# One-hot rows of a route ahead of its products, paired transposes for the logits, and other precedences in a planned kernel

## The chip, the core and the metric

The kernel runs on one core of a Trainium2 chip. The metric is the device time of one execution in microseconds (us). The engines of the core are TensorE (PE, matmuls), VectorE (DVE), ScalarE (ACT), GpSimd (POOL, which here gathers and scatters rows by index) and SyncE (SP, which here issues plain DMAs and DMA transposes). Each engine takes its own list of instructions strictly as the program puts it down, and waits on semaphores for the others.

## The reference, cut to what is computed

A convolution with softmax weights over 7 positions, then a mixture of 8 experts with the two best of each token, then a mixture with the best one. There are 2 x 3584 = 7168 tokens of width 192, and 1024 hidden columns.

```python
def _attn_ref(x, weight_gen):                     # x (2, 3584, 192), weight_gen (2, 3584, 8, 7)
    w = np.exp(weight_gen - np.max(weight_gen, axis=-1, keepdims=True))
    w = w / (np.sum(w, axis=-1, keepdims=True) + 1e-09)
    ...
    return np.einsum('bshk,bskhg->bshg', w, x_unf).reshape(B, S, D)

def _moe_ref(x, w_gate, w_noise, noise, w1, w2):
    noisy_logits = x @ w_gate + np.log1p(np.exp(x @ w_noise)) * noise
    top2 = np.argpartition(-noisy_logits, 2, axis=1)[:, :2]
    ...
            h = np.maximum(x[mask] @ w1[e], 0.0)
            out[mask] += top2_w[mask, k, None] * (h @ w2[e])

def _moe2_ref(x, w_gate, w1, w2):
    expert_idx = np.argmax(x @ w_gate, axis=1)
    ...
        out[mask] = gate_w[mask, None] * (np.maximum(x[mask] @ w1[e], 0.0) @ w2[e])
```

## The kernel before

**Phases and blocks.** Tokens are held in tiles of 128 rows. The expert work is split into five phases: phases 0 to 2 are the first mixture (the tokens in three parts), phases 3 and 4 the second (two parts). Within a phase the tokens of an expert are packed into blocks of 128 rows, and one or two blocks make a unit. A unit is a gather on POOL (`gt<-rows,src`: rows by index into SBUF), a DMA transpose on SP (`xt<-gt`), and then on PE, for each block, the first layer (`ph`, 40 matmuls of 128 columns, or 40 of 256 for two blocks) and the second (`py`, 24 matmuls of 192 columns). Between them ACT makes `hh` and DVE makes `hl` (high and low part of the hidden values, one `hl` for each 512 values of `ph`). The result `yo` is scattered by POOL, to `ybuf` in the first mixture and to `out_dram` in the second. `w` holds weights that are copied in for blocks whose expert is known only at run time, `wres` the resident ones.

**The route.** Before a phase can start, its route has to know where each token goes: `msk` (one-hots of the chosen expert), two products and two scans over it, a block and a place for each token, and then the inversion, token numbers by place. The inversion is a sum of one-hot products: for groups of 8 columns (`OG` = 8) DVE makes `pex` (the place as a one-hot row) and `bex` (the block as one, times a code; two instructions), and PE multiplies them into `pr`. From `pr`, after a product with `lost`, come `src` (the row numbers for POOL's gathers), then `ge` and the block's experts. `pex` and `bex` have two buffers each (`EB` = 2). The function is `route_`, the loop is that over `groups`.

**Logits.** Before a route come the logits of its tokens. A sub is up to four tiles of 128 rows. When its rows are final (`finish` for the convolution, `settle` after the first mixture), they are stored to memory and queued. `turn_thread` has SP transpose the rows two tiles at a time (`TPN` = 2) into `xtg`, of which there are three (`XR` = 3), and `logit_thread` multiplies them by the gate's weights on PE (`pm`). The function of a sub's convolution is `conv_lane`, which ends in `finish`.

**The order.** All this is written as generators ("threads") under one planner, `Feed`. After each step of PE's main loop it asks each thread when its next step could start by a model of the engines' clocks, adds a number of the thread's own ("late", negative for precedence), and takes the smallest. A thread tells what its step needs with `yield engine, tiles`: the step then counts as ready when the engine is free and the tiles are. The planner runs when the program is built. What it decides is the fixed order of every engine's list. `started` is filled when the first phase begins its expert work; all that is ahead of it is called the start here.

## Time and profile before

| | |
|---|---|
| median of 3 executions | 1036.34 us |
| lowest, highest | 1026.44, 1036.35 us |
| the profiled execution | 1031.08 us |
| its span | 1029.3 us |
| mean granted TensorE clock | 0.936 of full speed |

The span is the profiled stretch of one execution; some 1.8 us of the execution lie around it. All rows below come from that one execution, which is 5.3 us quicker than the median of the three and 4.6 us slower than the lowest. A row names a line, an engine, an operation, and out<-in by the program's names; L189 is a helper that records every instruction, so that nearly all have its line and the names tell them apart. In the timeline the brackets at the end of a row hold the engine's idle time ahead of it and what ended that.

### The profile page before, as it was taken

The page shows a single profiled execution, that of the slowest core. Times are in us where ns is not written, and L with a number is a line of the kernel's source. Part 1 is how long each engine was busy: PE and PEld are TensorE (multiplying, and loading weights), DVE is VectorE, ACT ScalarE, POOL GpSimd, SP SyncE. Part 2 cuts the span into 40 slices and gives each one's busy share as a digit, 9 for nine tenths or more (in the row PEclk, how much of TensorE's full clock was granted, in tenths as well). Part 3 has the DMA queues.
Part 4 walks back from the last instruction along what each step waited for, and adds up shares of the span by engine and source line. Part 5 has one row for each costly group of instructions (what it writes and reads, how often), then busy time and mean ns, then how long its engine had stood idle before and what let it go on. Part 6 is the DMA issues. An engine that isn't in the chain of part 4 may idle for free. (4 is left out here: it accounts for less than half of the span.)

```text
span 1029.3 us, 26213 instructions
## 1 busy us (share of the span) xinstructions
PE 885.5 (86%) x10130; PEld 816.2 (79%) x10130; DVE 741.6 (72%) x1818; ACT 500.9 (49%) x1003; POOL 424.5 (41%) x575
## 2 busy tenths in 40 slices
PE   1995369999995999999679999998399999999985
PEld 0553259989995899999579988998298998999985
DVE  7686859899985998958565767758686879355442
ACT  1343049674441544556255876865084733344332
POOL 3020044555525455533343444443145544465542
PEclk8897579999997999999889999999599999999998
DMA  9256089979843877644499999995289876563592
GB/s 286 54 137 150 0 164 261 220 191 177 188 87 77 155 146 168 172 103 134 118 159 254 261 232 236 245 254 98 59 183 198 194 149 200 112 121 87 176 255 82
DMA packets 246369, 168.30 MB, mean 164 GB/s; under 512 B 177564, under 2 KB 228079, under 8 KB 246236
## 3 DMA queue, kind: packets, MB, share of 16 engines
q1 hardware_dynamic: 227500, 121.68, 53.3%
q0 software_dynamic: 18736, 44.85, 18.0%
q8 instruction: 83, 1.36, 0.6%
q14 instruction: 50, 0.41, 0.2%
HBM read 74.46 MB, written 32.59 MB: 104 GB/s over the span
## 5 line engine op out<-in xcount | busy, mean ns | idle before, releaser
L189 ACT ACTIVATE hh<-ph 128x512 f16<-128x512 f32 x362 | 214.3, 594 | 344.6 <-PE ph L189 303.1
L189 PE MATMUL ph<-xt,wres 128*128 128x256 f16 (+1 forms) x3200 | 327.1, 255 | 31.1 <-DMA xt<-gt 19.6
L189 DVE SCALAR_TENSOR_TENSOR hl<-ph,hh 128x512 f16<-128x512 f32 x362 | 245.3, 685 | 136.7 <-ACT hh L189 132.2
L189 PEld LDWEIGHTS <-wres 128*128 128x128 f16 x3200 | 266.2, 100 | 53.1 <-issue 29.7
L189 PE MATMUL py<-wres,hh 128*128 128x192 f16 x2048 | 271.9, 246 | 4.7 <-ACT yo L189 4.6
L189 PEld LDWEIGHTS <-hh 128*128 128x128 f16 x2896 | 261.6, 98 | 13.8 <-issue 8.9
L189 POOL DMA_INDIRECT gt<-rows,src x181 | 195.4, 1079 | 155.3 <-DVE wmx L189 72.6
L189 PE MATMUL py<-wres,hl 128*128 128x192 f16 x1024 | 251.9, 246 | 0.0
L189 POOL DMA_INDIRECT ybuf<-yo,dest x120 | 131.7, 1097 | 275.9 <-ACT yo L189 261.6
L189 PE MATMUL ph<-xt,w 128*128 128x128 f16 (+1 forms) x1600 | 137.2, 240 | 22.1 <-DMA xt<-gt 9.3
L189 PEld LDWEIGHTS <-hl 128*128 128x128 f16 x1448 | 141.8, 98 | 0.0
L189 PEld LDWEIGHTS <-w 128*128 128x128 f16 x1600 | 116.7, 100 | 29.5 <-issue 8.5
L189 PE MATMUL py<-w,hh 128*128 128x192 f16 x848 | 113.8, 247 | 2.1 <-DMA w<-wres 2.0
L189 POOL DMA_INDIRECT out_dram<-yo,dest x61 | 62.4, 1022 | 122.6 <-ACT yo L189 71.8
L189 PE MATMUL py<-w,hl 128*128 128x192 f16 x424 | 104.8, 247 | 0.0
L189 PE MATMUL acc<-prod,identf 128*128 128x384 f32 x168 | 62.2, 529 | 13.4 <-DVE prod L189 9.6
L189 PEld LDWEIGHTS acc<-prod,identf 128*128 128x128 f32 x168 | 33.9, 207 | 35.7 <-DVE prod L189 11.0
L189 DVE COPY w<-wres 128x3072 f16 x53 | 51.5, 975 | 12.6 <-issue 6.0
L189 ACT ACTIVATE yo<-py 128x192 f32<-128x192 f32 x120 | 37.2, 327 | 35.9 <-PE py L189 17.3
L189 DVE SCALAR_TENSOR_TENSOR wres<-w,wsc,wres 128x1024 f16<-128x1024 f32 (+1 forms) x32 | 49.4, 1545 | 3.6 <-ACT wres L189 3.6
L189 ACT ACTIVATE wres<-w,wsc 128x1024 f16<-128x1024 f32 (+1 forms) x32 | 43.5, 1358 | 12.7 <-DVE wsc L189 9.2
L189 DVE TENSOR_TENSOR acc<-acc,tmp 128x768 f32<-128x768 f32 (+1 forms) x60 | 47.9, 798 | 2.1
(201 smaller groups left out, 827.7 us busy)
## 6 DMA issues: line engine op xcount, KB each, us to landing
w<-wres SPq DMA_DIRECT2D x23, 768.0 KB
rows<-rows SPq DMA_DIRECT2D x24, 512.0 KB
w<-in_moe_w_dram SPq DMA_DIRECT2D x14, 768.0 KB
w<-in_moe_w_dram SPq DMA_DIRECT2D x13, 512.0 KB
xs<-in_x_dram SPq DMA_DIRECT2D x6, 960.0 KB
rows<-ybuf SPq DMA_DIRECT2D x10, 384.0 KB
yl<-ybuf SPq DMA_DIRECT2D x10, 384.0 KB
wres<-wbt SPq DMA_DIRECT2D x56, 64.0 KB
```

Source lines behind the costliest of these rows:

```text
L189: return fn(*args, **kw)
```

## The change

It changes three things. In `route_` the loop over groups makes the one-hot rows of up to two groups before it emits the products of the first of them; the step in which it makes them no longer names the two buffers as needed. In `turn_thread` the second transpose of a sub follows the first at once, without a step of its own in between, once the first phase has started. And the threads for logits get a "late" of -2.0 after that point (0.0 before), as `finish` does (`FLATE`, where it had the number of its lane).

```diff
-LLATE = 0.0
+LLATE = -2.0
 RLATE = -4.0
+FLATE = -2.0
...
                 xt = rt.tile([P, 4 * TPN, P], F16, name="xtg", bufs=XR)[:, 0:4 * k]
-                yield "S", rows, xt
+                if not a or not started:
+                    yield "S", rows, xt
                 SP.dma_start_transpose(xt, rows.bitcast(F16)[:, a:a + k].rearrange("p t c -> p (t c)"))
...
-            feed.add(finish(r, acc, t0, n, busy, on_pe + (ln > 0), t), lane_th[ln][2])
+            feed.add(finish(r, acc, t0, n, busy, on_pe + (ln > 0), t), FLATE if started else lane_th[ln][2])
...
-        for k, (reg, c0, n) in enumerate(groups):
+        def sums(hot):
+
+            (reg, c0, n), oh, ob = hot
+            for v in range(n):
+                PE.matmul(tp[:, reg * nb:(reg + 1) * nb], oh[:, :, v], ob[:, :, v],
+                          start=(c0 % 16 + v == 0), stop=(c0 % 16 + v == 15 or c0 + v == nw - 1))
+
+
+        made = []
+        for reg, c0, n in groups:
             lo = c0 % 16
+            if len(made) == EB:
+                yield ("P",) + made[0][1:]
+                sums(made.pop(0))
             oh = rt.tile([P, P, OG], F16, name="pex", bufs=EB)[:, :, 0:n]
             ob = rt.tile([P, nblkm, OG], F16, name="bex", bufs=EB)[:, 0:nb, 0:n]
-            yield "V", oh, ob
+            yield "V",
...
-            yield "P", oh, ob
-            for v in range(n):
-                PE.matmul(tp[:, reg * nb:(reg + 1) * nb], oh[:, :, v], ob[:, :, v],
-                          start=(lo + v == 0), stop=(lo + v == 15 or c0 + v == nw - 1))
+            made.append(((reg, c0, n), oh, ob))
+        while made:
+            yield ("P",) + made[0][1:]
+            sums(made.pop(0))
...
-    logit_ths = [feed.add(turn_thread(), LLATE), feed.add(logit_thread(), LLATE)]
+    logit_ths = [feed.add(turn_thread()), feed.add(logit_thread())]
...
+    for th in logit_ths:
+        th[2] = LLATE
```

Nothing differs in any engine's list up to the point where the first phase starts. Behind it the lists hold the same work in another order. Three places follow.

**POOL, from phase 0 to phase 1.** `ybuf<-yo` are the scatters of phase 0's last blocks, `gt<-rows_66` the gathers of phase 1, `spacer` a small write that separates them. Before:

```order
L189 DMA ybuf_68<-yo,dest 9216x192
L189 MEMSET spacer 1x1
L189 DMA ybuf_68<-yo,dest 9216x192
L189 DMA gt<-rows_66,src 128x256 x10
L189 MEMSET spacer 1x1
```

After, the first eight gathers stand ahead of the last of these scatters:

```order
L190 DMA ybuf_68<-yo,dest 9216x192
L190 DMA gt<-rows_66,src 128x256 x8
L190 MEMSET spacer 1x1
L190 DMA ybuf_68<-yo,dest 9216x192
L190 DMA gt<-rows_66,src 128x256 x2
```

On PE the first `ph` of phase 1 moves with them ahead of the last 24 `py` of phase 0.

**DVE, from phase 2 to phase 3.** `blkh` is the block of each token as a number, from which `bex` is made; `pex` and `bex` are the one-hot rows; `hl` belongs to phase 2's expert work. Before, the whole route stands in one piece at the end of phase 2:

```order
L189 TENSOR_SCALAR sli<-sli 128x36
L189 CAST blkh<-sli 128x36
L189 TENSOR_TENSOR pex<-ipx,posh 128x1024
L189 TENSOR_TENSOR bex<-ipx,blkh 128x344
L189 TENSOR_TENSOR bex<-bex,code 128x344
L189 TENSOR_TENSOR pex<-ipx,posh 128x1024
```

After, the one-hot rows of two groups stand together and `hl` between the pairs:

```order
L190 CAST blkh<-sli 128x36
L190 SCALAR_TENSOR_TENSOR hl<-ph,hh 128x512
L190 TENSOR_TENSOR pex<-ipx,posh 128x1024
L190 TENSOR_TENSOR bex<-ipx,blkh 128x344
L190 TENSOR_TENSOR bex<-bex,code 128x344
L190 TENSOR_TENSOR pex<-ipx,posh 128x1024
L190 TENSOR_TENSOR bex<-ipx,blkh 128x344
L190 TENSOR_TENSOR bex<-bex,code 128x344
L190 SCALAR_TENSOR_TENSOR hl<-ph,hh 128x512
```

The route's `msk` has moved ahead by 11 `hl` of expert work, and the first four groups of products stand ahead of PE's last `py` of phase 2 instead of behind it.

**POOL, from phase 3 to phase 4.** `out_dram<-yo` are scatters of phase 3, `gt<-rows_65` gathers. Here the first gathers of phase 4 are the two in one row before:

```order
L189 DMA out_dram<-yo,dest 7168x192
L189 DMA gt<-rows_65,src 128x260 x2
L189 MEMSET spacer 1x1
L189 DMA out_dram<-yo,dest 7168x192
L189 DMA gt<-rows_65,src 128x260
L189 MEMSET spacer 1x1
L189 DMA out_dram<-yo,dest 7168x192
L189 DMA gt<-rows_65,src 128x260
```

After, those four gathers stand together, behind two more scatters:

```order
L190 DMA out_dram<-yo,dest 7168x192
L190 MEMSET spacer 1x1
L190 DMA out_dram<-yo,dest 7168x192
L190 MEMSET spacer 1x1
L190 DMA out_dram<-yo,dest 7168x192
L190 DMA gt<-rows_65,src 128x260 x4
L190 MEMSET spacer 1x1
```

On PE, 80 `ph` and 48 `py` stood between the route's `lost` product and the first `ph` of phase 4 before. After, 12 `py` stand there.

## Rows read from the trace of the kernel before

**Rows 1.** The page: PE's busy time (section 1) and one costly group (section 5).

```profile
...
PE 885.5 (86%) x10130; PEld 816.2 (79%) x10130; DVE 741.6 (72%) x1818; ACT 500.9 (49%) x1003; POOL 424.5 (41%) x575
...
L189 DVE SCALAR_TENSOR_TENSOR hl<-ph,hh 128x512 f16<-128x512 f32 x362 | 245.3, 685 | 136.7 <-ACT hh L189 132.2
...
```

**Rows 2.** PE's waits, whole span: releaser, us in total, times, longest.

```profile
...
PE ph L189 <- DMA xt<-gt: 28.9, 5, 10.7
PE pr L189 <- DVE bex L189: 23.3, 10, 11.4
PE pm L189 <- DMA xtg<-rows: 15.1, 8, 7.8
...
```

**Rows 3.** The chain of waits: start, duration, a piece of phase 2.

```profile
...
615.81 0.99 PE py L189 x12
616.80 1.12 PE ph L189 x20
...
```

**Rows 4.** PE's timeline, phase 0 to 1: start, duration, [idle before].

```profile
...
320.72 0.45 PE L189 MATMUL pr<-rb,lost 39*128 39x88 f32 x2
331.90 2.29 PE L189 MATMUL ph<-xt,wres 128*128 128x256 f16 x10 [10.73 <-DMA xt<-gt]
...
```

**Rows 5.** POOL's timeline, phase 0 to 1.

```profile
...
321.53 0.97 POOL L189 DMA_INDIRECT ybuf<-yo,dest  x1 [0.22 <-issue]
323.83 0.98 POOL L189 DMA_INDIRECT gt<-rows,src  x1 [1.33 <-DVE segt L189]
...
```

**Rows 6.** PE's timeline, phase 1 to 2.

```profile
...
488.73 1.23 PE L189 MATMUL pr<-bex,pex 128*128 128x72 f16 x8
...
496.13 0.25 PE L189 MATMUL py<-w,hl 128*128 128x192 f16 x1
504.71 4.09 PE L189 MATMUL ph<-xt,w 128*128 128x128 f16 x40 [8.33 <-DMA xt<-gt]
```

**Rows 7.** DVE's timeline, phase 1 to 2.

```profile
...
492.45 0.23 DVE L189 CUSTOM_DVE_ANT_0 src<-rb,rc 128x144 uint16<-128x144 uint16 x1
...
```

**Rows 8.** POOL's timeline, phase 1 to 2.

```profile
...
496.16 0.98 POOL L189 DMA_INDIRECT gt<-rows,src  x1 [0.30 <-issue]
...
```

**Rows 9.** PE's waits in 530 to 720 us, most of phase 2.

```profile
...
PE pm L189 <- DMA xtg<-rows: 5.3, 4, 2.3
...
```

**Rows 10.** PE's timeline, phase 2 to 3.

```profile
...
717.51 0.25 PE L189 MATMUL py<-wres,hl 128*128 128x192 f16 x1
...
730.38 0.84 PE L189 MATMUL pr<-bex,pex 128*128 128x43 f16 x8 [0.34 <-DVE bex L189]
...
732.82 1.27 PE L189 MATMUL pr<-bex,pex 128*128 128x43 f16 x12 [0.40 <-DVE bex L189]
742.24 2.29 PE L189 MATMUL ph<-xt,wres 128*128 128x128 f16 x20 [8.14 <-DMA xt<-gt]
...
```

**Rows 11.** DVE's timeline, phase 2 to 3.

```profile
...
711.72 0.37 DVE L189 CAST msk<-oh 128x288 f16<-128x288 f32 x1
...
```

**Rows 12.** POOL's timeline, phase 2 to 3.

```profile
...
736.11 0.98 POOL L189 DMA_INDIRECT gt<-rows,src  x1 [16.27 <-DVE segt L189]
...
```

**Rows 13.** PE's timeline, phase 3 to 4.

```profile
...
866.04 0.41 PE L189 MATMUL pr<-rb,lost 14*128 14x42 f32 x2
...
875.22 1.29 PE L189 MATMUL ph<-xt,wres 128*128 128x128 f16 x20
878.47 0.33 PE L189 MATMUL py<-w,hh 128*128 128x192 f16 x2 [1.96 <-DMA w<-wres]
...
```

**Rows 14.** POOL's timeline, phase 3 to 4.

```profile
...
868.29 0.98 POOL L189 DMA_INDIRECT gt<-rows,src  x1 [0.41 <-DVE segt L189]
...
875.99 1.01 POOL L189 DMA_INDIRECT out_dram<-yo,dest  x1 [1.86 <-ACT yo L189]
...
```

**Rows 15.** One stretch: busy time of PE, PEld, DVE, ACT, POOL; then granted clock.

```profile
...
506.00:508.00 2.00, 2.00 (x22) 2.00 (x20) 0.28 (x1) 0.60 (x1) 0.01 (x1) 0.50 0.31 93
...
```

**Rows 16.** The waits of SP, whose instructions issue DMAs.

```profile
...
SPq L189 <- PE pm L189: 21.3, 12, 6.2
...
```

## The prediction, made before the changed kernel ran

> **What bounds the kernel now.** I read the page first: PE is busy for 885.5 of 1029.3 us [rows 1], so that most of the time is matmul work that the change doesn't touch, and only PE's idle time can be won. Next, what ends that idle time [rows 2]: 28.9 us for transposed rows (`xt`), 23.3 for one-hot rows (`bex`), 15.1 for transposes for the logits (`xtg`). Then the timelines, to place these waits. They lie at the borders between phases, where a phase's first gather needs the route. Three borders have a stall before, and one has none: 10.73 us from phase 0 to 1 [rows 4], 8.33 from 1 to 2 [rows 6], and 24.5 from 2 to 3, from the last `py` (717.51 + 0.25) to the first `ph` (742.24), of which short products filled a part [rows 10]. From 3 to 4 the first `ph` at 875.22 shows no idle time [rows 13]. Inside a phase PE runs nearly without gaps. There a move in the order costs or gives nothing, as long as nobody waits.
>
> To place a moved instruction I count the matmuls between it and a neighbour in PE's order and price them: 20 `ph` of 128 columns take 1.12 us and 12 `py` 0.99 [rows 3]. A block of 128 rows has 40 `ph` and 24 `py`, 2.24 + 1.98 = 4.2 us.
>
> **Start.** Same order, 0.
>
> **Border 0 to 1.** The gather that releases the first `ph` starts at 323.83, after `src`, with POOL just done with a scatter that began at 321.53 and took 0.97 [rows 5]. In the new order the last product groups stand some 6 us of PE work earlier, and the gathers ahead of the last scatter. But they stay behind the scatter ahead of that, which ended at about 321.3 (POOL was idle for 0.22 ahead of 321.53), so a gather can start at about 321.6 at the earliest: 2.2 us won. Against it, 24 `py` (2 x 0.99 = 2.0 us) of phase 0 now stand behind the first `ph` of phase 1 and run after the stall instead of ahead of it. PE's idle time begins 2 us earlier, and the `ph` comes 2.2 earlier: **-0.2 us**. The bounds are -1 (the route's chain is done sooner than the scatter) and +1 (the gather stays behind DVE's `src`).
>
> **Border 1 to 2.** Here the order goes the other way. SP's loads for the convolution stand behind more `xt`, the last logits of this part come later, and the last group of products, at 488.73 before [rows 6], is now PE's last instruction of phase 1, behind the `py` that ended at 496.38. Before, it ended at 489.96, and DVE had `src` at 492.45 + 0.23 [rows 7], 2.7 us behind. The first gather, 496.16, waited for scatters and not for `src` [rows 8]. Now `src` comes 2.7 us after 496.4, at 499.1, and the gather 0.3 later (POOL's usual step, the bracket of [rows 8]) at 499.4: **+3.2 us**. Bounds +2 (DVE is free of other work by then) and +5 (the chain meets an `hl` or two of 0.69 us [rows 1] and the scatters behind).
>
> **Transposes for logits, phase 2.** PE waits 5.3 us for `xtg`, in four waits of at most 2.3 [rows 9]; the other waits of the 15.1 lie elsewhere, the longest with 7.8 [rows 2]. With both transposes issued together the second should land sooner; the planner puts the reading earlier too, with a precedence of -2, so that PE may get to it before the data does. I take **-1**, with -5 (all in phase 2 goes) and +4 (as many waits as before, each near the 2.3) as bounds.
>
> **Border 2 to 3, the part that gains.** Before, `msk` starts at 711.72 [rows 11] and the first gather at 736.11 [rows 12], 24.4 us of DVE in one piece, nearly all behind PE's last `py`. Now `msk` stands 21.4 us of PE work earlier, at about 690.3. DVE has 24.4 us of route and 11 `hl` of 0.685 [rows 1], 7.5 us, before `src`: 690.3 + 31.9 = 722.2. PE: the four groups of products that now stand ahead of the last `py` take 0.84 each [rows 10], 3.4 us, and I allow 1 us of waiting for the first `bex`, which is due within a microsecond of PE's arrival. The last `py` then ends at 717.8 + 3.4 + 1 = 722.2. Behind it stand four matmuls (a third of the 1.27 us that twelve took, 0.4) and the way from the last product to the gather, which was 736.11 - 734.09 = 2.0 before. The gather starts at 724.6, 11.5 earlier; I take **-11**. Bounds -12 (no wait for `bex`) and -8 (DVE falls three microseconds behind, since PE's `hl` now queue between its one-hot rows). The pair of one-hot groups in front of an `hl` costs it twice 1.22 us (the distance of two product groups, which DVE paced [rows 10]); that is hidden as long as PE has a block of 4.2 us to go on with, which in phase 2 it has.
>
> **Border 3 to 4, the part that loses.** Before, the gather came 2.25 us after `lost` (868.29 [rows 14] against 866.04 [rows 13]) and the first `ph` 6.93 after the gather; 80 `ph` and 48 `py`, 4.5 + 4.0 = 8.4 us, covered these 9.2. Now only 12 `py`, 0.99 us, are left as cover, and the gathers stand behind two more scatters. The scatter of the block that ended just before the first `ph` began at 875.99 and took 1.01 [rows 14], so the gather starts 0.8 + 1.0 + 0.3 = 2.1 us after PE runs dry, and the `ph` 6.93 later: a new stall of 9.0 us. The wait of 1.96 us for `w` that followed [rows 13] falls into it: **+7.0 us**. Bounds 5.4 (the way from gather to `ph` as short as the 6.13 at the border before, 742.24 - 736.11) and 9 (the wait for `w` stays).
>
> **The clock.** Before, the granted clock is 0.50, the lower level of 1.2 GHz, in the stretch behind the stall at 1 to 2 [rows 15], and 40 `ph` there take 4.09 us [rows 6], against 2.24 at 1.12 per 20 [rows 3]. A fourth stall of that kind brings a fourth such restart: **+2**, between 0 and 2.5. The stalls that only get shorter (2 to 3, from 24.5 to about 8.5) keep theirs. The Trainium skill, "TensorE: Matmul & The Clock Gate", section "HAM oscillation — how this bites in real kernels", says the same from the other end: each wait that lets the gate close makes the work behind it start at the lower level again, so many separate waits cost more than one long one. That rule speaks against this change, which splits 11 us off one stall and makes another of 9; without it the sum would be 2 us lower.
>
> **Sum.** 0 - 0.2 + 3.2 - 1 - 11 + 7.0 + 2 = 0.0 us, 1031.1 against the profiled execution's 1031.08. That execution is 5.3 us below the median, so the same change on the median gives 1036.3. The middle of the two is 1033.7: I say **1034**. The low ends of all terms sum to -10.6 and the high ends to +13.5. The three times before lie within 1% of one another, and 1%, about 10 us, is what a measurement of this kernel can tell from no change.
>
> **Rival A: the low ends.** The gain at 2 to 3 comes in full, the new stall at 3 to 4 lies at its lower bound without a half-speed restart, and the waits for `xtg` in phase 2 vanish, with the other two terms at their low ends too: -10.6 us, 1023 from the same middle. For it: the routes and the logits do get precedence, and a phase 3 that starts 11 us sooner moves nothing else later. Against it: the cover of 0.99 us at the last border is fixed by PE's order, and no speed elsewhere restores it.
>
> **Rival B: SP is held up, and the kernel is slower.** The second transpose of a sub goes to SP's list with no step that waits for a free `xtg`. SP takes its list in order, so if PE hasn't read the buffer yet, SP stands still, and every `xt` behind it too. Before, SP waited 12 times for `pm`, 21.3 us in all and 6.2 at most [rows 16], with no loss on PE inside phase 2 beyond that in [rows 9]. It decides when a hold outlasts what PE has to go on with, in phase 2 mostly a unit of two blocks, 8.4 us. If six subs hold it for 10.6 us (1.7 times the longest hold now), PE loses 2.2 six times, 13 us: 1047. For it: there are three buffers and two are taken by each sub. Against it: the planner still counts free `xtg` before it lets a transpose go, and the logits that free them are earlier too. The Trainium skill, "DMA: Bandwidth & Descriptors", section "Anatomy of one DMA — SWDGE (gpsimd) path", says that a wait on a semaphore is done by the issuing sequencer ahead of dispatch and not by the DMA engines; this rival is that rule, and the waits of [rows 16] agree with it.
>
> **Rival C: half of the gain.** DVE is the bound at 2 to 3: the pairs of one-hot groups put 2.4 us in front of an `hl`, PE waits for it, and the products move ahead by half of what the order says. The gain is 6 instead of 11, the sum +5.0, 1039. For it: DVE's 722.2 and PE's 722.2 are equal, so there is no slack between them.
>
> **How the numbers follow.** Chances: my forecast 0.52 (its own range 1028 to 1039), A 0.20, C 0.14, B 0.14. The range 1021 to 1044 holds the forecast, C and most of A, and leaves out B beyond its lower half. Faster by over 1% (under 1026) comes nearly all from A: 0.20. Slower by over 1% (above 1047) is half of B and the tail of the forecast and C: 0.13. Within 1%: 0.67.
>
> **What would show it.** In the changed kernel's timeline: at 2 to 3 product groups ahead of the last `py` and a first `ph` some 8.5 us behind it (13 us or more: C), at 3 to 4 an idle time of about 9 us that ends with `xt`, with a granted clock of 0.5 behind it (none: A), at 1 to 2 a first `ph` about 11.5 us after the last `py`, where it was 8.3. SP's waits for `pm` over 40 us, with PE waiting for `xt` inside a phase, would be B. I am wrong most easily in the 3 to 4 term, if the order of two engines there hides a wait that I have not seen, and in the execution-to-execution spread of 10 us, which is as large as any single term.

## The result, and the profile after

The changed kernel takes 1041.09 us (median of 18 executions, 1037.52 to 1046.05), the kernel before 1031.45 us beside it (18, 1023.61 to 1036.61). The ratio is 1.0097 with a 95% interval of 1.0076 to 1.0118: slower by one per cent. The profiled execution took 1038.51 us with a span of 1036.6, 7.3 us more than before. The forecast was no change, 0.0 us.

PE's busy time rose by 5.6 us against [rows 1], with the same number of instructions; more of them ran at the lower clock level, as the stretches further down show. PE's waits, below, answer to [rows 2]: the wait for one-hot rows halved (23.3 to 12.3), that for `xt` grew (28.9 to 33.5), and three lines grew or are new, for `w` (7.4 before, on the same view), `ge` and `hl`.

```profile
...
PE 891.1 (86%) x10130; PEld 821.2 (79%) x10130; DVE 741.3 (72%) x1818; ACT 499.4 (48%) x1003; POOL 431.3 (42%) x575
...
```

```profile
...
PE ph L190 <- DMA xt<-gt: 33.5, 4, 10.9
PE pr L190 <- DVE bex L190: 12.3, 7, 9.6
...
PE ph L190 <- DVE w L190: 9.9, 7, 4.9
...
PE pm L190 <- DMA xtg<-rows: 7.7, 6, 2.4
...
PE pr L190 <- DVE ge L190: 4.3, 1, 4.3
PE ph L190 <- DVE hl L190: 3.3, 2, 2.9
...
```

The line for the logits' transposes (`xtg`) fell from 15.1 to 7.7, but nothing was won there. The longest of these waits, 7.8 us, lies in the start, whose order is the same in both kernels; the view puts it down to `xtg` in one execution and to `ra` in the other. Without it the line is 7.3 before and 7.7 after. The kernel before, then the changed one:

```profile
...
97.49 0.20 PE L189 MATMUL pm<-gwh,xtg 128*128 128x16 f16 x1 [7.79 <-DMA xtg<-rows]
...
```

```profile
...
96.62 0.20 PE L190 MATMUL pm<-gwh,xtg 128*128 128x16 f16 x1 [7.89 <-DVE ra L190]
...
```

**Where the time went.** The first `ph` of each phase is easy to find in PE's timeline, so I cut both executions there. A second profile of the changed kernel (e12 below) gives the spread of one execution to the next. All in us; "end" is the end of the last `py`.

| from first `ph` of ... to that of ... | before | changed | difference | changed, second profile | difference |
|---|---|---|---|---|---|
| span's start to phase 1 | 331.90 | 330.86 | -1.0 | 335.10 | +3.2 |
| phase 1 to 2 | 172.81 | 176.73 | +3.9 | 176.85 | +4.0 |
| phase 2 to 3 | 237.53 | 230.84 | -6.7 | 234.12 | -3.4 |
| phase 3 to 4 | 132.98 | 142.49 | +9.5 | 142.40 | +9.4 |
| phase 4 to end | 144.61 | 146.27 | +1.7 | 146.24 | +1.6 |
| sum | 1019.83 | 1027.19 | +7.4 | 1034.71 | +14.9 |

The terms for 1 to 2, 3 to 4 and phase 4 repeat to 0.1 us; the start and the inside of phase 2 differ by 3 to 4 us between two executions of the same order. The 24 `py` that moved behind the first `ph` of phase 1 (2.0 us at the price of [rows 3]) stand in the first line before and in the second after. Border 1 to 2 itself so costs 1.9 and 2.0 us, and the first line grew by 1.0 and 5.2.

**Border 1 to 2**, PE's timeline of the changed kernel, with a row 37 us further on. The first `ph` comes 11.5 us after the last `py`, where it was 8.3 [rows 6], and 10.5 us after the last product, which now stands behind that `py` (it begins at 495.88 and takes 1.23; the wait for `ge` is the first part of the stall).

```profile
...
501.38 0.18 PE L190 MATMUL pr<-ge,ones 16*128 16x32 f16 x1 [4.28 <-DVE ge L190]
507.59 3.95 PE L190 MATMUL ph<-xt,w 128*128 128x128 f16 x40 [6.02 <-DMA xt<-gt]
516.41 2.31 PE L190 MATMUL ph<-xt,w 128*128 128x128 f16 x20 [4.88 <-DVE w L190]
...
544.31 1.65 PE L190 MATMUL ph<-xt,wres 128*128 128x256 f16 x10 [2.87 <-DVE hl L190]
...
```

In DVE's timeline of the same stretch `src` is ready at 499.6 + 0.23, 7.2 us later than in [rows 7], and POOL's first gather starts at 500.11 instead of 496.16 [rows 8]. Then DVE stands 7.02 us at an instruction on `m` (the two best logits' weights), and the copies of `w` that PE's second block needs come behind it:

```profile
...
499.60 0.23 DVE L190 CUSTOM_DVE_ANT_0 src<-rb,rc 128x144 uint16<-128x144 uint16 x1
...
512.12 0.18 DVE L190 TENSOR_SCALAR m<-m 128x20 f32<-128x20 f32 x1 [7.02 <-ACT m L190]
...
514.53 1.83 DVE L190 COPY w<-wres 128x3072 f16 x2
...
```

What it waits for is on ACT: the exponential of `m` is queued behind `hh`, which waits for the first `ph`, that is for the stall itself. Further on ACT stands again, 6.26 us, until SP has passed a branch around a block that is rarely run (line 1606):

```profile
...
509.96 0.60 ACT L190 ACTIVATE hh<-ph 128x512 f16<-128x512 f32 x1 [13.50 <-PE ph L190]
...
511.87 0.22 ACT L190 ACTIVATE m<-m 128x20 f32<-128x20 f32 x1
...
542.94 1.09 ACT L190 ACTIVATE hh<-ph 128x512 f16<-128x512 f32 x2 [6.26 <-SPq L1606]
...
```

SP came late there: two transposes for the logits in a row held it for 5.30 us ahead of that branch:

```profile
...
535.67 5.30 SPq L190 DMA_TRANSPOSE xtg<-rows  x2
...
```

**The first part of phase 2.** To compare the inside of phase 2 I count the columns of its `ph` and `py` (the second number of a row's shape); they are 428,032 in all in each of these runs. The first 90,000 of them, 300 `ph` and 203 `py`, take 51.6 us before and 56.9 and 57.0 in the two profiles of the changed kernel: 5.3 us more. PE's busy time, the first number behind the comma, is 44.4 of 51.6 us before and 46.3 of 56.9 after, so that 3.4 us are idle time and 1.9 slower work. Before, then after:

```profile
...
504.71:556.31 51.60, 44.40 (x517) 42.33 (x518) 27.85 (x67) 24.45 (x56) 17.23 (x25) 0.90 0.94 193
...
```

```profile
...
507.59:564.49 56.90, 46.31 (x538) 43.47 (x539) 32.09 (x91) 25.99 (x60) 17.62 (x25) 0.88 0.82 182
...
```

**Border 2 to 3** answers to [rows 10 to 12]. `msk` starts 11.2 us earlier on the clock; four groups of products stand ahead of the last `py`, which ends at 729.9; the stall from there to the first `ph` is 8.5 us, where it was 24.5. DVE, PE and POOL:

```profile
...
700.55 0.36 DVE L190 CAST msk<-oh 128x288 f16<-128x288 f32 x1
...
```

```profile
...
722.00 0.82 PE L190 MATMUL pr<-bex,pex 128*128 128x43 f16 x8
...
729.48 0.33 PE L190 MATMUL py<-wres,hh 128*128 128x192 f16 x2
...
729.73 0.49 PE L190 MATMUL pr<-bex,pex 128*128 128x43 f16 x4
...
738.43 0.82 PE L190 MATMUL ph<-xt,wres 128*128 128x128 f16 x6 [8.07 <-DMA xt<-gt]
```

```profile
...
732.27 0.97 POOL L190 DMA_INDIRECT gt<-rows,src  x1 [0.71 <-DVE segt L190]
...
```

**Border 3 to 4** answers to [rows 13, 14], where PE had no stall. PE runs dry at 872.4, POOL's scatter begins 0.8 us later, the gather 2.1 us after it runs dry, and the `ph` another 6.5 later:

```profile
...
870.89 0.41 PE L190 MATMUL pr<-rb,lost 14*128 14x42 f32 x2
...
880.92 2.31 PE L190 MATMUL ph<-xt,wres 128*128 128x128 f16 x20 [8.53 <-DMA xt<-gt]
...
```

```profile
...
873.18 0.97 POOL L190 DMA_INDIRECT out_dram<-yo,dest  x1 [5.06 <-ACT yo L190]
874.46 0.98 POOL L190 DMA_INDIRECT gt<-rows,src  x1 [0.30 <-issue]
...
```

The view of stretches gives the granted clock as the third number from the end. It is at the lower level, 0.50, behind this stall, and for a shorter time behind the stop that ends at 544.31:

```profile
...
543.60:545.60 2.00, 1.29 (x10) 1.04 (x10) 1.83 (x10) 0.42 (x1) 0.00 (x0) 0.86 0.69 165
545.60:547.60 2.00, 2.00 (x14) 1.85 (x13) 1.90 (x8) 1.68 (x4) 0.00 (x0) 0.50 1.20 82
547.60:549.60 2.00, 2.00 (x18) 1.72 (x17) 1.07 (x2) 0.20 (x1) 0.00 (x0) 0.79 0.82 182
881.00:884.00 3.00, 3.00 (x26) 2.72 (x27) 0.53 (x4) 0.60 (x1) 0.00 (x0) 0.50 0.26 58
...
```

### The profile page after: what moved, and what is told of

Its sections match the earlier page's. It is cut to its first block, busy times and chain, and to the rows that moved or that the text cites. A ratio compares the mean times of both kernels' runs of the same rounds, so it can differ in the third digit from the quotient of the medians.

```text
span 1036.6 us, 26210 instructions
## 1 busy us (share of the span) xinstructions
PE 891.1 (86%) x10130; PEld 821.2 (79%) x10130; DVE 741.3 (72%) x1818; ACT 499.4 (48%) x1003; POOL 431.3 (42%) x575
## 3 DMA queue, kind: packets, MB, share of 16 engines
q1 hardware_dynamic: 227500, 121.68, 50.9%
## 5 line engine op out<-in xcount | busy, mean ns | idle before, releaser
L190 PE MATMUL py<-wres,hh 128*128 128x192 f16 x2048 | 274.7, 247 | 4.9 <-ACT yo L190 4.8
L190 POOL DMA_INDIRECT ybuf<-yo,dest x120 | 136.2, 1135 | 280.3 <-ACT yo L190 265.2
L190 DVE COPY w<-wres 128x3072 f16 x53 | 51.6, 978 | 14.3 <-issue 7.5
L190 PEld LDWEIGHTS acc<-prod,identf 128*128 128x128 f32 x168 | 33.7, 206 | 35.3 <-DVE prod L190 10.6
L190 ACT ACTIVATE wres<-w,wsc 128x1024 f16<-128x1024 f32 (+1 forms) x32 | 43.5, 1359 | 12.3 <-DVE wsc L190 9.2
```

Source lines behind the costliest of these rows:

```text
L190: return fn(*args, **kw)
```

## The experiments

Each ratio is to the kernel before, with its 95% interval. "Phase 1 to 2", "2 to 3" and so on are the distances of the table above, from each run's own profile.

**e1 and e11, one-hot rows alone.** The loop of `route_` as in the change, all else as before, timed twice.

```diff
-        for k, (reg, c0, n) in enumerate(groups):
+        made = []
+        for reg, c0, n in groups:
...
+            if len(made) == EB:
+                yield ("P",) + made[0][1:]
+                sums(made.pop(0))
```

> The kernel before with only the one-hot rows of two groups made ahead of the products. Theory 1 (the time is lost and won at the borders, by where each route's last logits and products land in PE's order): the last products of the route for phase 2 land behind phase 1's last work here too, so the first ph of phase 2 comes 3 to 8 us later; the route for phase 3 starts 10 us of PE work earlier but all its products still stand behind the last py, so border 2 to 3 shortens by some 9 us; the cover at border 3 to 4 falls from 8.4 to 6.5 us of work, plus 0 to 3 us. Sum: 1029 to 1035, ratio to before 0.998 to 1.004. Rival (the one-hot pairs hold up hl on DVE, which is what made the changed kernel slower): nearly the whole loss shows here, ratio 1.007 to 1.012, with PE waiting for hl many times inside phases.

> The kernel of e1 once more, since its median was 11 us above that of the kernel before while its profiled execution was only 2.5 us above. If e1's profiled execution was the typical one, ratio 0.998 to 1.006 now; if the median was, 1.010 to 1.016, and the profile of this run should show at which place the further 6 to 8 us lie (an execution of the same order with another wait, at a border or at a queue that is full).

Measured: 1.0137 (1.0108 to 1.0165) and 1.0122 (1.007 to 1.0173), so that the first median was the typical one and not the first profile. The expectation of theory 1 missed. The totals lie at or above the upper end of the rival's range, but its mechanism isn't there. Phase 1 to 2 took 175.7 and 176.5 (before 172.8), 3 to 4 took 136.8 and 136.7 (133.0); these two repeat and make some 7 us. Phase 2 to 3 took 233.1 in the first profile and 238.9 in the second. One wait in the second profile is as long as this difference of 5.8 us; the first has none of over 0.2 us at that place:

```profile
...
695.75 0.19 PE L189 MATMUL pm<-gwh,xtg 128*128 128x8 f16 x1 [5.94 <-DMA xtg<-rows]
...
```

So the same order gains 4 or loses 1 in phase 2, by whether a transpose for the logits lands in time. Of PE's many waits for `hl`, which the rival asked for, the first profile shows one, of 0.62 us.

**e2, the change without the one-hot rows.**

```diff
-            made.append(((reg, c0, n), oh, ob))
-        while made:
-            yield ("P",) + made[0][1:]
-            sums(made.pop(0))
+            yield "P", oh, ob
+            for v in range(n):
+                PE.matmul(...)
```

> The changed kernel with the loop over one-hot groups put back, so pairs of transposes and the precedences alone. Theory 1: the order up to the middle of phase 2 is nearly that of the changed kernel, so the first ph of phase 2 is 3 to 4 us late again and the wait for w behind it (4.9 us) is there too; border 2 to 3 keeps 8 to 11 us of its gain; at border 3 to 4 the route's lost product lands 11.8 us of PE work ahead of the first ph of phase 4 instead of 1.0, so the stall of 8.5 us there and its half-clock restart go. Sum: some 8 to 11 us faster than the changed kernel, ratio to before 0.996 to 1.003. Rival (one-hots on DVE): the loss at 1 to 2 goes as well and the gain at 2 to 3 stays, ratio 0.985 to 0.992.

Measured: 1.0046 (1.0017 to 1.0076), some 5 us better than the changed kernel, a little outside theory 1's range. Phase 1 to 2 took 175.9 and the wait for `w` behind it was 5.2: the transposes and the precedences make that loss without the one-hot rows, as theory 1 had it. Phase 2 to 3 took 234.1, and 3 to 4 took 131.8: with its route done 11.8 us of work ahead, phase 4 starts without a stall.

```profile
...
878.72 1.28 PE L190 MATMUL ph<-xt,wres 128*128 128x128 f16 x20
...
```

**e3, the precedences alone.**

```diff
-LLATE = 0.0
+LLATE = -2.0
+FLATE = -2.0
...
+    for th in logit_ths:
+        th[2] = LLATE
```

> The kernel before with only the precedences (logit threads and finish at -2). Theory 1: its order puts the last products of the route for phase 2 2 us of work later and all else about where it was before, so plus 0 to 3 us, ratio 0.999 to 1.004, with borders 2 to 3 and 3 to 4 as before; what moved the routes in the changed kernel is then the paired transposes. Rival (the precedence of -2 by itself makes PE wait for transposes and pushes other work back): ratio 1.006 or more, with PE's waits for xtg above 15 us.

Measured: 1.003 (0.9995 to 1.0064), no change, as expected. Phase 1 to 2 took 170.6.

**e10, the change without the pairs.**

```diff
-                if not a or not started:
-                    yield "S", rows, xt
+                yield "S", rows, xt
```

> The changed kernel without the pairs of transposes: one-hot rows ahead and the precedences. By its order the last products of the route for phase 2 land behind the last py and the block that is rarely run (as in e1), the route for phase 3 starts 13 us of PE work earlier than before with all products behind the last py, and the lost product for phase 4 has 11.8 us of cover. Theory 1: plus 4 to 6 us at 1 to 2, minus 5 to 9 at 2 to 3, 0 to plus 3 at 3 to 4: ratio 0.998 to 1.005. Rival (one-hot rows ahead cost time by themselves, beyond the borders, which the median of e1 at 1.014 hints at): ratio 1.008 to 1.016.

Measured: 1.0087 (1.0059 to 1.0114). Phase 1 to 2 took 175.5, 2 to 3 took 237.7, 3 to 4 took 136.0. Theory 1's total missed. The stall at 2 to 3 did get shorter, 17.0 us where it was 24.5, as expected; but from its first `ph` to its last `py` phase 2 took 220.8 us, 7.7 more than before, and that took the gain.

**e4 to e7, the combining earlier.** Four runs with the threads that feed the routes of phases 3 and 4 given precedence, to see whether the route for phase 4 is late by the planner's choice.

e4, on the changed kernel:

```diff
-C2LATE = 0.0
+C2LATE = -4.0
```

e5, on the changed kernel, for phase 4 alone; e6 has -1.0 for both phases, and e7 is as e6, but on e3:

```diff
-            feed.add(combine_lane(r, pools[0], k, r.subs), C2LATE)
+            feed.add(combine_lane(r, pools[0], k, r.subs), 0.0 if r.ph is phases[3] else -1.0)
-                feed.add(settle(r, t0, n), C2LATE)
+                feed.add(settle(r, t0, n), 0.0 if r.ph is phases[3] else -1.0)
```

> The changed kernel with the threads that combine a phase's results (loads of ybuf, sums, rows, and behind them the logits) at precedence -4 instead of 0. Theory 2 (the route for phase 4 is late in the changed kernel because the steps that feed it are put behind others by the planner, not because an engine is full): the routes for phases 3 and 4 are done 25 and 80 us of PE work ahead, so the stalls at 2 to 3 (8.1 us of idle time) and 3 to 4 (8.5 us) and their half-clock restarts (2 us each) go, against 0 to 6 us of new waits for hl while DVE does the combining: ratio to before 0.983 to 0.997, with the loss at 1 to 2 unchanged. Rival (DVE, ACT or SP is full there, and the combining takes its time from hl and from transposes): the two stalls come back as waits inside phases 2 and 3, ratio 1.003 to 1.015.

> The changed kernel with one number more: the threads that combine for phase 4 run at -1 instead of 0. The order up to phase 3 is that of the changed kernel; the route's lost product for phase 4 then lies 30 us of PE work ahead of the first ph of phase 4, instead of 1.0. Theory 1 (the changed kernel loses 13 us at border 3 to 4 because this cover is gone): the stall of 8.5 us, its restart at half clock and the waits ahead of it go, 10 to 13 us off the changed kernel, ratio to before 0.996 to 1.001. Rival (the work that feeds the route takes DVE, ACT and SP from phase 3's blocks, so PE waits for hl, w and xt instead): less than 4 us off the changed kernel, ratio 1.004 or more, with PE's waits for w or hl in phase 3 longer by what the border gives back. The combining ahead of the weights made e4 57 us slower; if that rule bites here too, more than that.

> The changed kernel with the combining threads of phases 3 and 4 both at -1. The route for phase 3 is then done 21 us of PE work ahead of the border and the one for phase 4 30 us ahead. Theory 1: the stall at 2 to 3 (8.1 us of idle time, 2 to 3 us of half clock) goes as well as that at 3 to 4: 18 to 24 us off the changed kernel, ratio 0.985 to 0.993. Rival, as e4 showed it: phase 3 now begins before the second mixture's weights are ready, PE waits for them, and with the combining ahead of them they come later still: slower than the changed kernel.

> The kernel before with the precedences alone (e3) and the combining threads of phases 3 and 4 at -1: no pairs of transposes, no one-hot rows ahead. Theory 1: border 1 to 2 is where it was before (no loss of 9), both later stalls go (24.5 us at 2 to 3 with its restart, nothing at 3 to 4): ratio 0.976 to 0.986. Rival: as for e6, PE waits for the second mixture's weights, so 1.00 or more.

Measured: e4 1.0566 (1.0534 to 1.0598), e5 1.0168 (1.0122 to 1.0214), e6 1.0128 (1.008 to 1.0176), e7 1.0139 (1.0074 to 1.0204). All theories' totals missed. The rivals' totals hold in e5 and e7; e6 lies above the changed kernel, but not clear of it, and e4 lies far above both of its ranges. e5 is the clearest: up to phase 3 its order is the changed kernel's, and with 30 us of cover the stall at 3 to 4 is gone, as theory 1 said. But PE now waits 14.2 us in phase 3 for the second mixture's resident weights, whose threads (at -0.1) were put behind the combining:

```profile
...
PE ph L190 <- DMA wres<-wbt: 14.2, 1, 14.2
...
```

```profile
...
894.71 1.28 PE L190 MATMUL ph<-xt,wres 128*128 128x128 f16 x20
...
```

In e6 and e7 it is the weights again, with the second mixture's logits behind them, although PE's waits for `xt` at border 2 to 3 are gone or at most 3.9 us there. With the largest step in precedence, in e4, this is at its worst; PE's waits over the whole kernel:

```profile
...
PE ph L190 <- DMA wres<-wbt: 15.5, 2, 7.9
...
PE pm L190 <- DVE lg L190: 12.6, 3, 6.0
...
```

**e9, weights ahead of the combining.**

With the lines of e5, on the changed kernel:

```diff
-W2LATE = -0.1
+W2LATE = -1.5
```

> The changed kernel with the second mixture's weight threads at -1.5 (instead of -0.1) and the combining for phases 3 and 4 at 0 and -1. The route for phase 4 has its lost product 8.7 us of PE work ahead of phase 4, as in the kernel before, and the weights go ahead of the combining; the route for phase 3 starts 15 us of PE work earlier than before, 6 later than in the changed kernel. Theory 1: the loss at 1 to 2 stays (8 to 9 us), border 2 to 3 gains 8 to 11, border 3 to 4 loses 0 to 3, no wait for resident weights: 8 to 12 us off the changed kernel, ratio to before 0.996 to 1.003. Rival (the waits only change place, as in e5): PE waits 5 us or more for wres or its scales in phase 3, ratio 1.006 or more.

Measured: 1.0094 (1.0051 to 1.0137). Phase 3 to 4 took 131.5, no loss, as expected, and no wait for `wres` of note. But 2 to 3 took 240.6. The stall there was 15.1 us, 9.4 shorter than before, as expected; phase 2 from its first `ph` to its last `py` took 225.5 us instead of 213.1, and that took the gain. Theory 1's total missed; the rival holds by its total, not by its waits.

**e8, the copies of `w` on other engines.**

```diff
-FE = "VSAS,ASAS,VVVV,VVVS,VVSV".split(',')
+FE = "VSAS,ASAS,VVAS,VVVS,VVSV".split(',')
```

> The changed kernel with the weights of phase 2's first four blocks (expert known at run time) copied by ACT and by a DMA of SP instead of DVE. The order up to phase 2 is that of the changed kernel, so the first ph of phase 2 is late by the same 4 us. Theory 3 (behind it another 5 us are lost because DVE stands 7.0 us at an instruction on m that waits for ACT, with the copies of w queued behind it): PE's wait of 4.9 us for w goes, and 50 us into phase 2 it is 3 to 5 us behind the kernel before instead of 8.7. The borders after that lie about where they did before (24 us at 2 to 3, none at 3 to 4), so the total is 1030 to 1038, ratio 1.000 to 1.007. Rival (the copies of w are late because their engine or the weights are, wherever they are issued): PE's waits for w in the first 30 us of phase 2 stay at 5 us or more.

Measured: 1.0169 (1.011 to 1.0229), far above theory 3's total. At its place theory 3 holds for the wait: PE's waits for DVE's `w` in the first 50 us of phase 2 fell from 6.7 us to 1.5 for ACT's (with one of 2.1 for a weight's transfer beside it), although DVE still stood at `m`, now for 9.3 us. The first 90,000 columns took 54.3 us, against 56.9 in the changed kernel and 51.6 before, so half of that loss came back. PE's idle time there fell by 5.6 us, from 10.6 to 5.0; its busy time rose by 3.0, at a mean granted clock of 0.82 instead of 0.88. PE's wait, DVE's, and the stretch:

```profile
...
PE ph L190 <- ACT w L190: 1.5, 1, 1.5
...
```

```profile
...
DVE m L190 <- ACT m L190: 9.3, 1, 9.3
...
```

```profile
...
506.72:561.02 54.30, 49.31 (x557) 44.95 (x558) 28.19 (x92) 34.41 (x66) 15.87 (x23) 0.82 0.99 242
...
```

What the kernel lost, it lost further on (phase 2 to 3 took 244.0), where its order had changed too.

**e12, the changed kernel's second profile.**

The kernel is the changed one as it is, with no edit.

> The changed kernel's own second profile. Theory 1: the same places to within 2 us: first ph of phase 2 3 to 4 us later than before, 8 to 9 behind 50 us into phase 2, 12 to 15 won at 2 to 3, 12 to 14 lost at 3 to 4. If one of these terms is missing, it belonged to that one execution and not to the order.

Measured: 1045.95 us, one execution. The borders repeat (511.95, 520.78, 746.07 and 888.47 answer to 507.59, 516.41, 738.43 and 880.92): the wait for `w` is 4.83 us where it was 4.88, the stall at 2 to 3 is 8.7 where it was 8.5, and phase 3 to 4 agrees within 0.1 us. One term missed its range: from 90,000 columns into phase 2 to the first `ph` of phase 3 the first profile of the changed kernel won 12.0 us on the kernel before, this one 8.8, where 12 to 15 was expected. The rest of phase 2 is so not fixed by the order alone.

```profile
...
511.95 4.00 PE L190 MATMUL ph<-xt,w 128*128 128x128 f16 x40 [6.08 <-DMA xt<-gt]
520.78 2.31 PE L190 MATMUL ph<-xt,w 128*128 128x128 f16 x20 [4.83 <-DVE w L190]
...
```

```profile
...
746.07 2.31 PE L190 MATMUL ph<-xt,wres 128*128 128x128 f16 x20 [8.20 <-DMA xt<-gt]
...
```

```profile
...
888.47 2.31 PE L190 MATMUL ph<-xt,wres 128*128 128x128 f16 x20 [7.86 <-DMA xt<-gt]
...
```

**e13 to e15, the change behind border 1 to 2 only.** If the loss came from the first mixture's part of the change alone, these should win.

e13 is the kernel before with this edit; e14 is e13 with the lines of e5 at -0.05 for both phases.

```diff
-                yield "S", rows, xt
+                if not a or not started or r.m == 0:
+                    yield "S", rows, xt
```

e15 is e14 with the new loop of one-hot rows for phase 3 alone, and the logit threads at -2.0 from phase 2 on.

```diff
+        if ph is phases[3]:
...
+            made = []
+            for reg, c0, n in groups:
...
+            for th in logit_ths:
+                th[2] = -2.0
```

> The kernel before with only the pairs of transposes, and only for the logits of the second mixture. The order up to the route for phase 2 is word for word that of the kernel before; the route for phase 3 starts 8.6 us of PE work earlier, and the lost product for phase 4 has 13.0 us of cover instead of 8.7. Theory 1 (the loss at 1 to 2 comes from what the pairs and the one-hot rows do to the first mixture's order; the gain at 2 to 3 from the second mixture's logits): nothing lost at 1 to 2, 6 to 8 us won at 2 to 3, 0 at 3 to 4: ratio to before 0.991 to 0.997. Rival (the gain at 2 to 3 only feeds waits further on, as the waits for xtg in phase 2 or for weights in phase 3): 0.998 to 1.006.

> As e13, with the combining threads at -0.05 instead of 0, still behind the weights at -0.1. The route for phase 3 starts 18 us of PE work earlier than before and a third of its products stand ahead of the last py; the lost product for phase 4 has 6.5 us of cover instead of 8.7. Theory 1: 0 at 1 to 2, 12 to 15 us won at 2 to 3, 2 to 4 lost at 3 to 4: ratio 0.988 to 0.994. Rival (as in e5 and e6, the border's time comes back as waits for the second mixture's weights or logits): 0.998 or more, with waits for wres, its scales or xtg of 5 us or more in phases 2 and 3.

> As e14, with the logit threads at -2 from the start of phase 2 and the one-hot rows ahead for the route of phase 3 alone: all parts of the change, but only behind border 1 to 2. By its order the route for phase 3 starts 6.5 us of PE work earlier than before, the lost product for phase 4 has 11.8 us of cover. Theory 1: 0 at 1 to 2, 5 to 7 us won at 2 to 3, 0 at 3 to 4: ratio 0.992 to 0.998. Rival: as for e13.

Measured: e13 1.0013 (0.999 to 1.0035), e14 1.0077 (1.0048 to 1.0107), e15 1.0046 (1.0018 to 1.0073). Phase 1 to 2 took 170.3, 171.8 and 171.8, so that loss is indeed gone. But none is faster: by the totals the rivals hold. In e13 PE arrives later at border 2 to 3 (its last `py` ends at 725.2 instead of 717.8) and waits less for one-hot rows, 5.66 us instead of 11.41, and the first `ph` of phase 3 comes at 744.00, 237.2 us after that of phase 2 (237.5 before):

```profile
...
730.89 0.87 PE L189 MATMUL pr<-bex,pex 128*128 128x43 f16 x8 [5.66 <-DVE bex L189]
...
744.00 1.23 PE L189 MATMUL ph<-xt,wres 128*128 128x128 f16 x10 [8.17 <-DMA xt<-gt]
```

In e15 one wait for `hl` takes 10.4 us of phase 2; the stall at 2 to 3 got shorter by 5.2. This is not one of the waits that the rival named. DVE itself stood 15.60 us at an instruction ahead of that `hl`, and the view shows nothing that it waited for. PE's wait and DVE's idle time:

```profile
...
PE ph L189 <- DVE hl L189: 10.4, 1, 10.4
...
```

```profile
...
681.38 0.17 DVE L189 TENSOR_REDUCE ss<-lg 128x4 f32<-128x32 f32 x1 [15.60 <-issue]
...
```

## Why the prediction was wrong

**The step that failed** is the sum over phase 2. The prediction says that inside a phase "a move in the order costs or gives nothing, as long as nobody waits"; it costed border 1 to 2 through its first gather, and what moves behind that gather on DVE, ACT and SP at nothing. The gather term itself was right: counted from the first `ph` of phase 1 and without the 24 `py`, the gather starts 3.0 us later in both profiles (+3.2 forecast), though the first `ph` comes only 1.9 and 2.0 later, as it followed the gather after 7.5 us instead of 8.6. So was the border at 2 to 3: a first `ph` 8.5 us behind the last `py` was forecast, and 8.5 and 8.7 came. Set against 24.5 before, and with the 3.4 us of products that moved ahead of the `py`, that is 12.5 us won (forecast 11). But from the first `ph` of phase 2 to its last `py`, 213.1 us before, the changed kernel takes 222.3 and 225.4. Of the 9.2 and 12.4 more, 3.4 are the products; 6 and 9 are waits and half-clock work that no term held. The forecast had +1 for `bex` and -1 for `xtg`. Stretch by stretch, border 1 to 2 came out 1.3 and 1.2 us better than forecast, phase 2 with the border behind it 5.3 and 8.6 worse (-12 forecast, -6.7 and -3.4 measured), and phases 3 and 4 2 worse.

The measured time, 1041.09, does lie in the stated range of 1021 to 1044, but not because the mechanism was right: no change was forecast, and the kernel lost 9.6 us. Rival C's time, 1039, is close, but its sign, 13 us or more between the last `py` of phase 2 and the first `ph` of phase 3, didn't come.

**What stood in its place.** The first 90,000 columns of phase 2 take 5.3 us more in both profiles, and that is nearly all of the 6 us in the first and over half of the 9 in the second. Two chains are in it, and some slower work. In the first, `m` waits on ACT behind a `hh` that waits for the stall, DVE's copies of `w` wait behind `m`, and PE waits for `w`. e8 confirms that this makes PE's wait: it goes with the copies. But the kernel before waits for `w` in that stretch too, 5.6 us in all against 6.7, so on balance this chain adds 1.1 us of waiting. What the change moved is the exponential of `m`: before, it stands ahead of that `hh` and runs before the stall ends:

```profile
...
495.90 0.22 ACT L189 ACTIVATE m<-m 128x20 f32<-128x20 f32 x1
...
507.09 0.60 ACT L189 ACTIVATE hh<-ph 128x512 f16<-128x512 f32 x1 [10.30 <-PE ph L189]
...
```

The second is the stop at the branch: SP is held 5.3 us by two transposes, ACT stands 6.3, PE 2.9, and PE falls to half clock. The kernel before waits 1.6 us at this branch, so PE's two waits there, 0.35 and 2.87, add 1.6; the rest of the 3.4 us of idle time is a wait of 0.7 for `hl`. That the pair of transposes makes this stop is not shown. In e13 a pair (of the second mixture's logits) stands ahead of the branch too, with 1.90 and 2.77 us on SP; ACT stands 4.5 us there, and PE waits 1.8, about as long as in the kernel before. In e8, with the pair, PE waits 0.7. This is rival B's mechanism in a small form at most, at one place and behind a branch, not through full `xtg` buffers: SP's waits for `pm` went from 21.3 us [rows 16] to 19.2, and nowhere near 40.

**Border 0 to 1.** The stall is 10.9 and 10.6 us long where it was 10.7, so the term came out at +0.2 and -0.1 for the -0.2 forecast, but not by its mechanism. The gather was to start sooner; it starts 3.2 us after PE runs dry, where it was 2.7. The two scatters ahead of it wait for results of the last `py`, and these now stand behind the route's products.

**Border 3 to 4.** The stall was forecast at 9.0 us and is 8.5 and 7.9; with the restart at half clock (20 `ph` in 2.31 instead of 1.28 to 1.30) and waits of 0.4 to 2.0 us for `msk`, `w` and `bex` ahead of it, phases 3 and 4 together lose 11.1 us, against 9.0 forecast (7.0 and 2). Of this, 1.7 lie in phase 4, where a further stretch of the changed kernel runs at half clock (last section). e2 and e9 confirm the reason: with 9 to 12 us of cover again, phase 3 to 4 takes 131.5 to 131.8. The term's low bound of 5.4 doesn't follow from its own numbers: 2.1 + 6.13 - 1.96 is 6.3, so that rival A's sum would be -9.7.

**Transposes for the logits in phase 2.** -1 forecast, within -5 to +4. In the stretch of [rows 9] PE's waits for `xtg` were 5.3 us before, and 6.8 and 4.9 in the two profiles after. The other executions show how much this depends on one landing (e11).

**The clock** was weighed at 2 us. There are three more stretches at 0.50 than before: behind the new stall, behind the 2.9 us stop in phase 2, and behind a wait of 2.7 us in phase 4. PE's busy time is 5.6 us longer for the same number of instructions. The rule of the Trainium skill that the prediction weighed ("TensorE: Matmul & The Clock Gate", section "HAM oscillation — how this bites in real kernels") agrees with that in its direction.

**Which part does it.** The table holds, for each run's profile, phase 1 to 2 (without the 24 `py` where they moved), then phase 2: its first 90,000 columns, the whole from its first `ph` to its last `py`, the stall behind it, and the sum of these last two. All in us.

| run | parts in the first mixture | 1 to 2 | first 90,000 | to the last `py` | stall | 2 to 3 |
|---|---|---|---|---|---|---|
| before | none | 172.8 | 51.6 | 213.1 | 24.5 | 237.5 |
| changed | all | 174.7 | 56.9 | 222.3 | 8.5 | 230.8 |
| changed, again | all | 174.9 | 57.0 | 225.4 | 8.7 | 234.1 |
| e2 | pairs, precedences | 175.9 | 57.3 | 222.8 | 11.3 | 234.1 |
| e9 | all | 175.3 | 56.8 | 225.5 | 15.1 | 240.6 |
| e8 | all | 175.2 | 54.3 | 220.9 | 23.2 | 244.0 |
| e10 | one-hot rows, precedences | 175.5 | 51.7 | 220.8 | 17.0 | 237.7 |
| e1 | one-hot rows | 175.7 | 51.4 | 213.6 | 19.6 | 233.1 |
| e11 | one-hot rows | 176.5 | 51.4 | 221.0 | 17.9 | 238.9 |
| e3 | precedences | 170.6 | 52.4 | 214.6 | 23.1 | 237.7 |
| e13 | none | 170.3 | 51.0 | 218.5 | 18.8 | 237.2 |
| e14 | none | 171.8 | 50.9 | 222.2 | 11.8 | 234.0 |
| e15 | none | 171.8 | 51.0 | 222.0 | 19.3 | 241.3 |

Border 1 to 2 is longer with the one-hot rows, and with the pairs and precedences together; precedences alone don't do it. The 5 us in the first 90,000 columns go with the pairs. In all eight profiles with pairs in the first mixture (these five, e4, e5 and e6) DVE stands 6.8 to 9.3 us at `m`; in the other nine it doesn't wait there for 3 us or more. The pairs were not run in the first mixture without the precedences.

It isn't the whole loss, though, and my first theory falls there: e13 to e15 have neither of the two and aren't faster. In all rows but the first, phase 2 to its last `py` is longer than before, by 0.5 to 12.5 us, and the stall behind it is shorter, by 1.3 to 15.9; their sum lies from 6.7 us below the kernel before to 6.5 above. e4, e6 and e7 do without most of that stall, and paid for it with the weights. Why work for a route that is put ahead of phase 2's blocks lengthens that phase is not shown.

**What stays open**: which of the many small waits make phase 2 longer in e13 (PE's waits from 560 to 715 us sum to 8.9 us against 6.0 before, half of what is missing), why phase 2 differs by 3 to 6 us between two executions of one order, as in e1 and e11, beyond the one wait shown, and what DVE waited for in e15.

## What to carry to other kernels

A stall at a border is also slack: it takes up what the phase before lost, so a gain at the border is only real if the work pulled ahead doesn't lengthen that phase; here the stall shrank by 16 us and 2 to 3 by 3 to 7. Cost a moved step through every in-order queue that it enters, above all the instruction that waits for another engine and what is queued behind it; the gather was right here, and what the sum missed lay behind it: in `m`, which stood behind `hh` on ACT, and at a branch that several engines pass. Before a wait that a trace shows is called the cost of a change, look for the same wait in the kernel before: PE's 6.7 us for `w` were 5.6 there. And where four chains of a planner compete, a precedence for one is a delay for another: each of e4 to e9 removed the wait it aimed at and was slower than the kernel before all the same.

## What the runs showed of the hardware

A stop of PE of 2.9 us in the middle of dense work was followed by a granted clock of 0.86, 0.50 and 0.79 in the three stretches of 2 us from 543.6 on; in the four stretches ahead of them it was 1.00. The same happened behind the wait of 4.88 us for `w`: 1.00 from 511 to 513, 0.50 from 515 to 519, and the twenty `ph` at 516.41 took 2.31 us instead of 1.28 to 1.30. I had expected a restart at the lower level behind the long stalls only, and had costed the short waits inside phase 2 at their own length.

The length of a stop doesn't decide it in these traces. At one place in phase 4, where both kernels wait for the same transfer of `w`, the longer wait of the kernel before was not followed by a lower clock, 1.00 in the stretches from 978 to 988 us, and the shorter one of the changed kernel was: 0.94 from 987 to 989, 0.50 from 989 to 991, 0.71 from 991 to 993. Before, then after:

```profile
...
981.35 1.29 PE L189 MATMUL ph<-xt,w 128*128 128x128 f16 x20 [3.26 <-DMA w<-wres]
...
```

```profile
...
987.76 1.44 PE L190 MATMUL ph<-xt,w 128*128 128x128 f16 x20 [2.68 <-DMA w<-wres]
...
```
